# The first 128 rows of the last block's first product move in front of a branch, and the last expert's sums get a bank each

## The chip, the cores and the metric

The kernel runs on one core of one Trainium2 chip. A core has five engines that run side by side and wait for each other through semaphores: TensorE (PE, matrix products; its weight loads are shown as PEld), VectorE (DVE), ScalarE (ACT), GpSimd (POOL) and SyncE (SP, which issues transfers). PE writes its results into PSUM, a memory of eight banks of 2 KB for each of its 128 partitions; DVE and ACT read them there and write to SBUF, from which PE takes its operands. Each engine has an instruction stream of its own, so a branch in the program is a branch on every engine. The metric is the device time in microseconds (us) from start to end; lower is better.

## The reference, cut to what matters

Three stages follow each other: a recurrent attention over 2 x 768 tokens, a mixture of 8 experts with a limited capacity, and a last block that is applied to every token.

```python
def _moe_ref(x, w_gate, w1, w2, capacity):
    ...                                   # every token goes to the expert of its largest logit
    h = np.maximum(np.einsum('ecd,edf->ecf', disp, w1), 0.0)
    y = np.einsum('ecf,efd->ecd', h, w2)
    ...

def _moe2_ref(x, w_in, w_out, g_ln):      # x: 1536 x 384, w_in: 384 x 1024, w_out: 1024 x 384
    h = x @ w_in
    h_max = np.max(h, axis=-1, keepdims=True)
    e = np.exp(h - h_max)
    sm = e / (np.sum(e, axis=-1, keepdims=True) + 1e-09)
    solu = h * sm
    mu = np.mean(solu, axis=-1, keepdims=True)
    var = np.mean((solu - mu) ** 2, axis=-1, keepdims=True)
    ln = (solu - mu) / np.sqrt(var + 1e-06) * g_ln
    return (ln @ w_out).astype(np.float32)
```

## The kernel before, in words

Every float32 matrix is kept as a high and a low part, and a product is three products: high by high, high by low, low by high. The experts come one after the other. Each has up to 224 rows here (`W`), and its 1024 hidden columns are taken in four quarters, numbered `g` from 0 to 31 over the eight experts. `mm1(g)` makes a quarter of the hidden layer (`hps`), ACT and DVE split it into `hh` and `hl`, and `mm2(g)` adds that quarter's share to the expert's result `yps`: for each of the three blocks of 128 result columns (`dd`) six matmuls, 18 in all. `yps` of an expert is two PSUM tiles: one of two column blocks that share a bank, one of the third. After the fourth quarter ACT copies each tile to the high part of the result (line 820, `yThi`), and DVE subtracts to get the low part (line 821, `yTlo`). The result stands transposed, `yT`: `yThi2` and `yTlo2` hold the first two column blocks, `yThi1` and `yTlo1` the third.

Beside this, `decode_piece` turns the last block's weights, which arrive as 64-bit patterns, into high and low parts piece by piece on DVE and ACT (16 pieces; 0 to 7 are `w_in`, 8 to 15 `w_out`).

An expert with more than 224 tokens needs extra work, `overflow()`. It stands under an `if` on the largest count; with these inputs the branch goes around it. Line 1122 is that branch. On every engine the code ahead of it, the code under it and the code behind it lie one after the other, and on the way around each engine first runs a few semaphore instructions that stand for what the code under the `if` would have counted; engines that wait for results from ahead of the branch wait, behind it, for these counts too.

`solu_block()` stands behind the branch. It first decodes piece 15 (the last of `w_out`). Then it goes over 12 tiles of 128 rows, two tiles ahead with the first product: `h2(t)` is `x @ w_in` for tile `t`, 18 matmuls of 512 columns; `norm1(t)` finds the row's maximum (line 989, DVE); `norm2(t)` is the exponential (line 1001, ACT), the weighting (line 1007, DVE) and the centring (line 1012, POOL); `norm3(t)` is the variance; `flip(t)` transposes (line 1037, PE) and splits; `out2(t)` is the second product. Tile 0 has its maximum and exponential in two halves, from two tiles of one bank each; the other tiles have one tile of two banks, of which there are two in turn, so `h2(3)` cannot start before DVE has finished line 1007 of tile 1.

The order on each engine is the order in which the code is written. PE's first tiles behind the branch are h2(0), h2(1), h2(2), flip(0), h2(3), flip(1), out2(0), h2(4); DVE's are piece 15, norm1(0), norm2(0), norm1(1), norm2(1).

Of the kernel before, what the change touches and what calls it, by code (L numbers as in the profile page):

```python
# [8 lines left out]
F32 = mybir.dt.float32  # L9
# [10 lines left out]
N, DM, NE, DF = B * S, H * D, 8, 1024  # L20
# [3 lines left out]
KD = DM // 128  # L24
KF = DF // 128
W = 224
# [9 lines left out]
def rwkv_moe_solu_kernel(  # L36
# [31 lines left out]
    V, S, G, T = nc.vector, nc.scalar, nc.gpsimd, nc.tensor  # L68
# [32 lines left out]
    raw_t, w1s, w2s, xe = {}, {}, {}, {}  # L101
# [576 lines left out]
    def experts_and_solu():  # L678
# [6 lines left out]
        ps_b = mctx.enter_context(tc.tile_pool(name="ps_b", bufs=2, space=PSUM, **pt))  # L685
        ps_t = mctx.enter_context(tc.tile_pool(name="ps_t", bufs=4, space=PSUM, **pt))

        yT = [[ytp.tile([128, n, YW], F32R, name=f"yT{x}{n}") for n in (2, 1)] for x in ("hi", "lo")]
# [3 lines left out]
        def col(x, kk, sl):  # L692
            return yT[x][kk // 2][:, kk % 2, sl]
# [87 lines left out]
        al = slice(None)  # L781
        hq = {}
# [21 lines left out]
        def mm2(g):  # L804
            e, q = divmod(g, 4)
            if q == 0:
                yps[e] = [ps_b.tile([128, n, W], F32, tag=f"b{n}", name=f"yps{e}_{n}") for n in (2, 1)]
            if q == 1:
                starts_of[e] = reg(e) if e else 0
            for dd in range(KD):  # L810
                for f in range(2):
                    mm3(
                        yps[e][dd // 2][:, dd % 2], w2s[g], hq[g], (al, f, slice(dd * 128, dd * 128 + 128)), (al, f),
                        q == 0 and f == 0 and dd != 1, q == 3 and f == 1,
                    )
            if q == 3:
                start = starts_of.pop(e)
                for n, src in enumerate(yps.pop(e)):
                    hi, lo = (yT[x][n][:, :, bass.ds(start, W)] for x in range(2))
                    S.activation(hi, src, AF.Copy)  # L820
                    V.tensor_tensor(lo, src, hi.bitcast(F32), ALU.subtract)
            w2s.pop(g)
            hq.pop(g)

        def reg(j):
            return nc.values_load(
                starts_i[0:1, j:j + 1], engines=(ENG.Activation, ENG.DVE), min_val=0, max_val=N,
                skip_runtime_bounds_check_because="prefix sums of clipped counts",
            )
# [67 lines left out]
        for g in range(NQ + 2):  # L897
# [27 lines left out]
            if g % 2 == 0 and g:  # L925
                j = g // 2
# [38 lines left out]
        def h2(t):  # L965
            if t == 0:
                ps = [ps_t.tile([128, 512], F32, tag="t", name=f"h2_{t}_{j}") for j in range(2)]
                h2p[t] = ps
            else:
                ps = ps_b.tile([128, 2, 512], F32, tag="b", name=f"h2_{t}")  # L970
                h2p[t] = [ps.rearrange("p a f -> p (a f)")]
                ps = [ps[:, j] for j in range(2)]
            ts_ = slice(t * 128, (t + 1) * 128)
            for j in range(2):
                fs = slice(j * 512, (j + 1) * 512)
                for i, (x, w) in enumerate(((0, 0), (0, 1), (1, 0))):
                    for kk in range(KD):
                        T.matmul(  # L978
                            ps[j], col(x, kk, ts_), wi[w][:, kk, fs], start=not (i or kk), stop=i == 2 and kk == KD - 1,
                        )  # L980
# [78 lines left out]
        def solu_block():  # L1059
            nc.sync.dma_start(out=inv_sb, in_=inv.rearrange("(m p) o -> p m o", p=128)[:, :, 0])  # L1060
            for _ in decode_piece(2 * NP - 1):
                pass
            for t in range(-2, NM):
                if t + 2 < NM:
                    h2(t + 2)
                    norm1(t + 2)
                if t < 0:
                    norm2(t + 2)
                    continue
                for i in range(t + 1 if t else 0, min(t + 2, NM)):  # L1070
                    norm3(i)
                flip(t)
                if t + 2 < NM:
                    norm2(t + 2)
                if t:
                    out2(t - 1)
            out2(NM - 1)

        def overflow():
            load_ids(0, NE, 2, NB)  # L1080
            for e in range(NE):
                ost = reg(NE + e)
                wv = []
                for kind, src in ((1, w1), (2, w2)):
                    for hf in range(2):
                        t = rawp.tile([128, 1536], F32, tag="raw", name=f"ow{kind}_{e}_{hf}")
                        nc.sync.dma_start(out=t, in_=src[e, :, hf])
                        wv.append(t.rearrange("p (q a f) -> p q a f", q=2, a=4 - kind))
                for o in range(NOV):
                    xo = load_xe(e, 2 + o, 1)  # L1090
                    ps = ps_t.tile([128, KD, 128], F32, tag="t", name=f"oxt{e}_{o}")
                    for kk in range(KD):
                        T.transpose(ps[:, kk], xo[:, 0, kk * 128:(kk + 1) * 128], ident)
                    xt = xe_p.tile([128, KD, 128], F32, tag="xhi", name=f"oxs{e}_{o}")
                    V.tensor_copy(xt, ps)
                    hps = ps_b.tile([128, KF, 128], F32, tag="b", name=f"ohp{e}_{o}")
                    for f in range(KF):
                        for kk in range(KD):
                            w = wv[f // 4][:, f // 2 % 2, kk, f % 2 * 128:f % 2 * 128 + 128]
                            T.matmul(hps[:, f], w, xt[:, kk], start=kk == 0, stop=kk == KD - 1)  # L1100
                    ho = [h_p.tile([128, 4, 128], F32, tag="hh", name=f"oh{e}_{o}_{j}") for j in range(2)]
                    for j in range(2):
                        S.activation(ho[j], hps[:, 4 * j:4 * j + 4], AF.Relu)
                    yo = ps_t.tile([128, KD, 128], F32, tag="t", name=f"oy{e}_{o}")
                    for dd in range(KD):
                        for f in range(KF):
                            w = wv[2 + f // 4][:, f // 2 % 2, f % 2, dd * 128:dd * 128 + 128]
                            T.matmul(yo[:, dd], w, ho[f // 4][:, f % 4], start=f == 0, stop=f == KF - 1)
                    for n, sl in ((0, slice(0, 2)), (1, slice(2, 3))):
                        hi, lo = (yT[x][n][:, :, bass.ds(ost + 128 * o, 128)] for x in range(2))  # L1110
                        S.activation(hi, yo[:, sl], AF.Copy)
                        V.tensor_tensor(lo, yo[:, sl], hi.bitcast(F32), ALU.subtract)

        return overflow, solu_block, most

    with tc.manual_schedule():
# [62 lines left out]
```

## Time and profile before

| | us |
|---|---|
| median of 3 runs (339.26 to 340.45) | 340.26 |
| the profiled execution's own time | 340.68 |
| its span, from the first to the last instruction | 338.9 |
| PE busy in it | 321.2 (95%) |
| DVE, ACT, POOL busy | 244.2, 190.2, 145.0 |

The profiled execution is 0.42 us above the median of the runs; 1.8 us of it lie outside the span. Times in the rows below are microseconds from the start of the span.

### The profile page before, as it was taken

To read this page: it belongs to the slowest core of one execution; us is meant where nothing else is said; L and a number is where in the kernel's file an instruction comes from. 1 tells how busy PE (TensorE), PEld (TensorE's weight loads), DVE (VectorE), ACT (ScalarE), POOL (GpSimd) and SP (SyncE) were. 2 spreads that over 40 slices of the span, in tenths; PEclk is the share of its full clock that TensorE was granted. 3 is DMA by queue.
4 is the path that set the end of the run, shared out by engine and by line. 5 is a ranking of instruction groups with operands and counts; after the bars stand their busy time and mean duration, and the time that the engine had idled before them with its cause. 6 is when DMAs were issued, how large, how long until landed. Compare 5 with 4: busy or idle time off the path is not lost. (4 is left out here: it accounts for less than half of the span.)

```text
span 338.9 us, 7222 instructions
## 1 busy us (share of the span) xinstructions
PE 321.2 (95%) x2656; PEld 296.6 (88%) x2656; DVE 244.2 (72%) x573; ACT 190.2 (56%) x408; POOL 145.0 (43%) x197
## 2 busy tenths in 40 slices
PE   8999999999999999999999999699999999999990
PEld 3789878888989999999999999588999999999990
DVE  8999999978598989898999897345664444444410
ACT  1556547565559687777787776124644344443420
POOL 7889798851432231414140455304244233333321
PEclk9999999999999999999999999989999999999997
DMA  6988999211986988989888943100000000000010
GB/s 215 391 323 252 342 384 366 78 67 40 327 299 232 291 286 293 279 286 275 280 264 289 279 148 52 8 0 1 2 23 23 25 23 23 25 23 25 23 47 23
DMA packets 20251, 56.22 MB, mean 166 GB/s; under 512 B 6579, under 2 KB 8885, under 8 KB 20213
## 3 DMA queue, kind: packets, MB, share of 16 engines
q1 hardware_dynamic: 16772, 47.67, 40.0%
q0 software_dynamic: 3440, 8.06, 9.6%
q8 instruction: 21, 0.34, 0.4%
q14 instruction: 18, 0.14, 0.1%
HBM read 50.56 MB, written 5.16 MB: 164 GB/s over the span
## 5 line engine op out<-in xcount | busy, mean ns | idle before, releaser
L779 PE MATMUL yps<-hh,wlo 128*128 128x224 f32 x192 | 52.9, 276 | 0.3 <-DMA wlo<-in_w 0.3
L121 DVE TENSOR_TENSOR wlo<-raw,whi 128x768 fp32r<-128x768 f32 x57 | 52.4, 952 | 1.0 <-ACT whi L115 0.7
L777 PE MATMUL yps<-hh,whi 128*128 128x224 f32 x192 | 52.8, 275 | 0.0
L778 PE MATMUL yps<-hl,whi 128*128 128x224 f32 x192 | 52.6, 274 | 0.0
L115 ACT ACTIVATE whi<-raw 128x768 fp32r<-128x768 f32 x64 | 50.8, 840 | 0.0
L1012 POOL TENSOR_SCALAR e<-e,nmu 128x1024 f32<-128x1024 f32 x12 | 13.5, 1125 | 67.8 <-DVE nmu L1011 67.8
L989 DVE TENSOR_REDUCE nm<-h 128x1 f32<-128x1024 f32 (+1 forms) x13 | 14.8, 1140 | 33.9 <-PE h L978 33.9
L779 PEld LDWEIGHTS yps<-hh,wlo 128*128 128x128 f32 x192 | 36.9, 192 | 0.5 <-DMA wlo<-in_w 0.5
L778 PEld LDWEIGHTS yps<-hl,whi 128*128 128x128 f32 x192 | 36.9, 192 | 0.0
L777 PEld LDWEIGHTS yps<-hh,whi 128*128 128x128 f32 x192 | 36.9, 192 | 0.0
L119 POOL DMA_DIRECT2D wlo<-in_w x7 | 6.9, 984 | 69.7 <-ACT wlo L124 69.7
L1046 PE MATMUL o<-w_hi,shi 128*128 128x384 f32 x96 | 33.1, 345 | 0.0
L1048 PE MATMUL o<-w_hi,slo 128*128 128x384 f32 x96 | 32.2, 335 | 0.0
L1047 PE MATMUL o<-w_lo,shi 128*128 128x384 f32 x96 | 32.2, 335 | 0.0
L791 PE MATMUL hps<-xhi,whi 128*128 128x224 f32 x192 | 27.5, 278 | 0.4 <-issue 0.4
L791 PE MATMUL hps<-xlo,whi 128*128 128x224 f32 x192 | 26.7, 275 | 0.0
L791 PE MATMUL hps<-xhi,wlo 128*128 128x224 f32 x192 | 26.6, 274 | 0.0
L791 PEld LDWEIGHTS hps<-xhi,whi 128*128 128x128 f32 x192 | 24.2, 192 | 0.6 <-issue 0.5
L93 POOL DMA_INDIRECT xe<-xs,ids x16 | 17.8, 1115 | 15.4 <-DMA ids<-idx 11.3
L978 PE MATMUL h<-w_hi,yThi 128*128 128x512 f32 x72 | 21.3, 405 | 3.2 <-ACTq L1122 3.0
L791 PEld LDWEIGHTS hps<-xhi,wlo 128*128 128x128 f32 x192 | 24.0, 192 | 0.0
L791 PEld LDWEIGHTS hps<-xlo,whi 128*128 128x128 f32 x192 | 24.0, 192 | 0.0
(183 smaller groups left out, 790.2 us busy)
## 6 DMA issues: line engine op xcount, KB each, us to landing
raw<-in_w SPq DMA_DIRECT2D x32, 768.0 KB
kvr<-in_kvr SPq DMA_DIRECT2D x12, 576.0 KB
rkT<-in_rkT SPq DMA_DIRECT2D x12, 512.0 KB
w<-in_w_in SPq DMA_DIRECT2D x8, 384.0 KB
w<-in_w_out SPq DMA_DIRECT2D x8, 384.0 KB
wlo<-in_w POOLq DMA_DIRECT2D x7, 384.0 KB
xs<-xg SPq DMA_DIRECT2D x12, 192.0 KB
xe<-xs,ids POOLq DMA_INDIRECT x16, 5.9
```

The costliest lines, as they stand in the source:

```text
L93: nc.gpsimd.indirect_dma_start(out=t[0:n, b, :], out_offset=None, in_=xs[0:rows, :], in_offset=bass.IndirectOffsetOnAxis(ap=ids[0:n, e, c: ...
L115: S.activation(hi, raw, AF.Copy)
L121: V.tensor_tensor(lo, raw, hi.bitcast(F32), ALU.subtract)
L777: T.matmul(ps, w[0][ws], x[0][xsl], start=first, stop=False, skip_group_check=True)
L778: T.matmul(ps, w[0][ws], x[1][xsl], start=False, stop=False, skip_group_check=True)
L779: T.matmul(ps, w[1][ws], x[0][xsl], start=False, stop=last, skip_group_check=True)
L791: T.matmul(ps[:, f], w1s[g][i][:, kk, wf], x[j][:, kk], start=not (i or j or f or kk), stop=j == 1 and kk == KD - 1, skip_group_check=True,)
L978: T.matmul(ps[j], col(x, kk, ts_), wi[w][:, kk, fs], start=not (i or kk), stop=i == 2 and kk == KD - 1,)
L989: V.tensor_reduce(nms[j], ps, AX.X, ALU.max, negate=True)
L1046: T.matmul(ps, hi[:, f % 4], wo[0][:, f], start=f == 0, stop=False)
L1047: T.matmul(ps, hi[:, f % 4], wo[1][:, f], start=False, stop=False)
L1048: T.matmul(ps, lo[:, f % 4], wo[0][:, f], start=False, stop=f == KF - 1)
```

## The change

Three things are edited. For the last expert, `yps` becomes three tiles, each in a bank of its own (the third takes the second buffer of the tag `b2`), and each is evicted by itself: three copies on ACT and three subtractions on DVE where there were two. `h2(0)` is called at the end of `experts_and_solu()`, which is ahead of the branch, and no longer in `solu_block()`; its 18 matmuls go column block by column block of `yT` (`kk`), and within each alternate between the two result tiles, so that the last column block is read by the last six alone. The code under the `if` takes its PSUM from the other pool, as the two banks of h2(0) are now in use there. Nothing else moves: piece 15, `norm1(0)` and all that follows stay behind the branch.

```diff
         def mm2(g):
             e, q = divmod(g, 4)
             if q == 0:
-                yps[e] = [ps_b.tile([128, n, W], F32, tag=f"b{n}", name=f"yps{e}_{n}") for n in (2, 1)]
+                ns = (2, 1) if e < NE - 1 else (2, 1, 2)
+                yps[e] = [ps_b.tile([128, n, W], F32, tag=f"b{n}", name=f"yps{e}_{i}") for i, n in enumerate(ns)]
...
+            alone = e == NE - 1
             for dd in range(KD):
+                y = yps[e][dd][:, 0] if alone else yps[e][dd // 2][:, dd % 2]
...
             if q == 3:
                 start = starts_of.pop(e)
                 for n, src in enumerate(yps.pop(e)):
-                    hi, lo = (yT[x][n][:, :, bass.ds(start, W)] for x in range(2))
+                    if alone:
+                        src = src[:, 0]
+                        hi, lo = (yT[x][n // 2][:, n % 2, bass.ds(start, W)] for x in range(2))
+                    else:
+                        hi, lo = (yT[x][n][:, :, bass.ds(start, W)] for x in range(2))
                     S.activation(hi, src, AF.Copy)
                     V.tensor_tensor(lo, src, hi.bitcast(F32), ALU.subtract)
...
             ts_ = slice(t * 128, (t + 1) * 128)
+            if t == 0:
+                for kk in range(KD):
+                    for i, (x, w) in enumerate(((0, 0), (0, 1), (1, 0))):
+                        for j in range(2):
+                            T.matmul(
+                                ps[j], col(x, kk, ts_), wi[w][:, kk, j * 512:(j + 1) * 512], start=not (i or kk),
+                                stop=i == 2 and kk == KD - 1,
+                            )
+                return
...
             for t in range(-2, NM):
                 if t + 2 < NM:
-                    h2(t + 2)
+                    if t + 2:
+                        h2(t + 2)
                     norm1(t + 2)
...
+        h2(0)
         return overflow, solu_block, most
```

How the instructions stand on PE shows what moves. In the kernel before, the last matmuls of the last expert (the third column block of `mm2(31)`) stand right ahead of the branch:

```order
L778 MATMUL yps_1_3527<-hl_3589,whi_31_3546 128x224
L779 MATMUL yps_1_3527<-hh_3588,wlo_31_3547 128x224
L777 MATMUL yps_1_3527<-hh_3588,whi_31_3546 128x224
L778 MATMUL yps_1_3527<-hl_3589,whi_31_3546 128x224
L779 MATMUL yps_1_3527<-hh_3588,wlo_31_3547 128x224
L1122 COMPARE_AND_BRANCH
```

All of h2(0) stood behind the branch. In the changed kernel PE has 18 matmuls of h2(0) between that place and the branch (line 1140 now); the last nine of them and the branch are these, where `h_0_0` and `h_0_1` are the two result tiles:

```order
L985 MATMUL h_0_1_3667<-w_lo_1513,yThi_1507 128x512
L985 MATMUL h_0_0_3666<-w_hi_1511,yTlo_1509 128x512
L985 MATMUL h_0_1_3667<-w_hi_1511,yTlo_1509 128x512
L985 MATMUL h_0_0_3666<-w_hi_1511,yThi_1508 128x512
L985 MATMUL h_0_1_3667<-w_hi_1511,yThi_1508 128x512
L985 MATMUL h_0_0_3666<-w_lo_1513,yThi_1508 128x512
L985 MATMUL h_0_1_3667<-w_lo_1513,yThi_1508 128x512
L985 MATMUL h_0_0_3666<-w_hi_1511,yTlo_1510 128x512
L985 MATMUL h_0_1_3667<-w_hi_1511,yTlo_1510 128x512
L1140 COMPARE_AND_BRANCH
```

The last six of the 18 are the only ones that read the third column block (`yThi_1508`, `yTlo_1510`); behind the branch PE now goes on with h2(1).

ACT, ahead of the same branch, copied two tiles before (the `ISA` rows set the address from the expert's start, which is only known at run time):

```order
L826 TENSOR_LOAD starts_i
L820 ISA
L820 ACTIVATE yThi_1507<-yps_2_3526 128x2x224
L820 ISA
L820 ACTIVATE yThi_1508<-yps_1_3527 128x224
L1122 COMPARE_AND_BRANCH
```

In the changed kernel it copies three:

```order
L833 TENSOR_LOAD starts_i
L827 ISA
L827 ACTIVATE yThi_1507<-yps_0_3526 128x224
L827 ISA
L827 ACTIVATE yThi_1507<-yps_1_3527 128x224
L827 ISA
L827 ACTIVATE yThi_1508<-yps_2_3528 128x224
L1140 COMPARE_AND_BRANCH
```

The first copy now reads what the first six of PE's last 18 expert matmuls complete, the second what the next six complete; DVE's subtractions stand in the same way, three for two.

## Rows read from the trace of the kernel before

**Rows 1.** The page, part 1: busy us, share, instructions of each engine.

```profile
PE 321.2 (95%) x2656; PEld 296.6 (88%) x2656; DVE 244.2 (72%) x573; ACT 190.2 (56%) x408; POOL 145.0 (43%) x197
```

**Rows 2.** Windows: length, busy us (instructions) by engine, granted clock, DMA share, GB/s.

```profile
30.00:60.00 30.00, 28.60 (x376) 25.17 (x374) 27.87 (x95) 18.03 (x59) 25.03 (x27) 1.00 0.94 351
...
215.85:218.88 3.03, 0.00 (x0) 0.00 (x1) 1.87 (x5) 0.82 (x2) 0.00 (x0) 1.00 0.27 8
218.92:222.33 3.41, 3.41 (x8) 2.76 (x9) 1.67 (x3) 0.61 (x1) 0.00 (x0) 0.50 0.02 2
...
234.04:330.00 95.96, 95.96 (x533) 88.76 (x534) 44.52 (x85) 42.34 (x77) 33.27 (x47) 1.00 0.06 23
```

**Rows 3.** Timeline of PE around the branch: start, us, instruction, [idle before <- releaser].

```profile
213.78 0.27 PE L778 MATMUL yps<-hl,whi 128*128 128x224 f32 x1
...
214.90 0.28 PE L779 MATMUL yps<-hh,wlo 128*128 128x224 f32 x1
...
215.57 0.27 PE L779 MATMUL yps<-hh,wlo 128*128 128x224 f32 x1
218.88 1.64 PE L978 MATMUL h<-w_hi,yThi 128*128 128x512 f32 x3 [3.04 <-ACTq L1122]
...
224.72 0.84 PE L978 MATMUL h<-w_hi,yThi 128*128 128x512 f32 x3
```

**Rows 4.** Line 1122, the branch: sequencer instructions by engine, ns min/median/max, first to last start.

```profile
L1122 DVEq EVENT_SEMAPHORE  x2: 21/21/21, 217.6 to 217.7; - x2
L1122 ACTq EVENT_SEMAPHORE  x2: 17/17/17, 218.8 to 218.9; - x2
...
L1122 PEldq COMPARE_BRANCH  x1: 397/397/397, 213.7 to 213.7; - x1
...
L1122 ACTq COMPARE_BRANCH  x1: 68/68/68, 216.5 to 216.5; - x1
L1122 DVEq COMPARE_BRANCH  x1: 84/84/84, 216.9 to 216.9; - x1
```

**Rows 5.** Timeline of ACT around the branch.

```profile
216.03 0.82 ACT L820 ACTIVATE yThi<-yps 128x448 f32 x2 [5.58 <-PE yps L779]
220.04 0.61 ACT L871 ACTIVATE w_hi<-da,g_sb 128x384 fp32r<-128x384 f32 x1 [3.19 <-DVE da L864]
```

**Rows 6.** Timeline of DVE from the branch to tile 1's weighting.

```profile
216.61 0.92 DVE L821 TENSOR_TENSOR yTlo<-yps,yThi 128x448 f32 x2 [4.97 <-ACT yThi L820]
217.86 0.36 DVE L858 TENSOR_SCALAR da<-w 128x384 int32<-128x384 int32 x1 [0.33 <-DVEq L1122]
...
220.69 0.62 DVE L873 SCALAR_TENSOR_TENSOR w_lo<-da,g_sb,w_hi 128x384 fp32r<-128x384 f32 x1 [0.68 <-ACT w_hi L871]
...
224.92 0.69 DVE L989 TENSOR_REDUCE nm<-h 128x1 f32<-128x512 f32 x1 [1.39 <-PE h L978]
...
232.60 1.28 DVE L1007 SCALAR_TENSOR_TENSOR e<-e,es,h 128x1024 f32<-128x1024 f32 x1
```

**Rows 7.** Timeline of PE, then POOL, before h2(3).

```profile
232.88 1.04 PE L1037 MATMUL st<-ident,e 128*128 128x128 f32 x8
234.04 0.93 PE L978 MATMUL h<-w_hi,yThi 128*128 128x512 f32 x3
...
229.95 1.14 POOL L1012 TENSOR_SCALAR e<-e,nmu 128x1024 f32<-128x1024 f32 x1 [14.91 <-DVE nmu L1011]
```

**Rows 8.** Timeline of PE, then ACT, at an earlier expert's last quarter.

```profile
186.16 0.27 PE L779 MATMUL yps<-hh,wlo 128*128 128x224 f32 x1
...
186.55 1.03 ACT L820 ACTIVATE yThi<-yps 128x448 f32 x2 [0.15 <-PE yps L779]
```

**Rows 9.** Groups by shape, whole span: busy us, mean ns of one, idle before.

```profile
L989 DVE TENSOR_REDUCE nm<-h 128x1 f32<-128x512 f32 x2 | 1.4, 692 | 2.9 <-PE h L978 2.9
...
L821 DVE TENSOR_TENSOR yTlo<-yps,yThi 128x224 f32 x7 | 2.7, 382 | 0.0
...
L820 ACT ACTIVATE yThi<-yps 128x224 f32 x7 | 2.5, 358 | 0.7
```

More of the change, by code (lines that the diff above doesn't have):

```diff
@@ L806, in mm2 @@
             if q == 0:
-                yps[e] = [ps_b.tile([128, n, W], F32, tag=f"b{n}", name=f"yps{e}_{n}") for n in (2, 1)]
+                ns = (2, 1) if e < NE - 1 else (2, 1, 2)
+                yps[e] = [ps_b.tile([128, n, W], F32, tag=f"b{n}", name=f"yps{e}_{i}") for i, n in enumerate(ns)]
             if q == 1:
                 starts_of[e] = reg(e) if e else 0
+            alone = e == NE - 1
             for dd in range(KD):
+                y = yps[e][dd][:, 0] if alone else yps[e][dd // 2][:, dd % 2]
                 for f in range(2):
                     mm3(
-                        yps[e][dd // 2][:, dd % 2], w2s[g], hq[g], (al, f, slice(dd * 128, dd * 128 + 128)), (al, f),
-                        q == 0 and f == 0 and dd != 1, q == 3 and f == 1,
+                        y, w2s[g], hq[g], (al, f, slice(dd * 128, dd * 128 + 128)), (al, f),
+                        q == 0 and f == 0 and (alone or dd != 1), q == 3 and f == 1,
                     )
@@ L1090, in overflow @@
                     xo = load_xe(e, 2 + o, 1)
-                    ps = ps_t.tile([128, KD, 128], F32, tag="t", name=f"oxt{e}_{o}")
+                    ps = ps_b.tile([128, KF, 128], F32, tag="b", name=f"oxt{e}_{o}")[:, 0:KD]
                     for kk in range(KD):
@@ L1103, in overflow @@
                         S.activation(ho[j], hps[:, 4 * j:4 * j + 4], AF.Relu)
-                    yo = ps_t.tile([128, KD, 128], F32, tag="t", name=f"oy{e}_{o}")
+                    yo = ps_b.tile([128, KF, 128], F32, tag="b", name=f"oy{e}_{o}")[:, 0:KD]
                     for dd in range(KD):
```

## The prediction

> **What bounds the kernel now.** I read the page first: PE is busy for 95% of the span [rows 1], so only what keeps PE waiting, or slow, can matter. Then the windows: from 234.04 to 330 us PE is never idle [rows 2], so whatever moves the start of h2(3) moves the end by as much, and I need not look behind it. Then PE's timeline at the branch. The last expert matmul starts at 215.57, and the next matmul, the first of h2(0), at 218.88: 3.04 us idle, released by ACT's instructions of the branch line [rows 3]. In that gap the granted clock falls: the first 3.41 us behind it run at 0.50 (the 1.2 GHz level), and the eight matmuls that start there take 3.41 us [rows 2], 0.43 us each, where 36 matmuls of the same shape take 8.16 us from 224.72 to 232.88, 0.227 us each [rows 3, 7]. So the branch costs PE 3.0 us idle and some 1.7 us of half speed.
>
> The gap itself: PE's branch record is at 213.7, when the second of the last 18 matmuls starts (213.78), that is 17 matmuls, each with its weight load, ahead of execution [rows 3, 4]. ACT starts its two copies at 216.03 and ends at 216.85 [rows 5]; its branch record is at 216.5, and its first instruction behind it at 218.8, 2.3 us later [rows 4]. That is what PE waits for. DVE needs no more than 0.7 us, from 216.9 to 217.6 [rows 4].
>
> One thing there is odd, and I shall need it. Where no branch is near, ACT's copy of an expert's result starts 0.39 us behind the start of the last matmul that it needs (186.16 and 186.55) [rows 8]. At the branch the matmul is at 214.90 and the copy at 216.03, 1.13 us behind [rows 3, 5]. 216.0 is also 2.3 us after PE's branch record, the time that ACT's own branch takes. So PE may **hold back its semaphore updates** while it waits for the code behind its branch.
>
> **The change part by part.** *The three banks.* The third sum is complete with the same matmul as before. Its copy may start at 215.57 + 0.39 = 215.96, takes 0.36 and the subtraction 0.38 [rows 9], so DVE is free at 216.7 instead of 216.61 + 0.92 = 217.53 [rows 6]. The first two sums are complete 12 and 6 matmuls earlier, so their copies lie beside PE's work. One copy and one subtraction more cost ACT and DVE nothing that anyone waits for: ACT was idle for 5.58 us before them [rows 5].
>
> *h2(0) in front of the branch.* Its 18 matmuls follow the expert's at once, from 215.7. The third column block is read by the 13th to the 18th, from 215.7 + 12 x 0.227 = 218.4, and its copy and subtraction are done by then. At full clock they end at 215.7 + 18 x 0.227 = 219.8. PE's branch record comes 17 matmuls ahead again, as the second of the 18 is started, at 215.7 to 215.9; with 2.3 us its code is there at 218.2. ACT's record comes with its third copy at 216.0, its code at 218.3. Both lie under h2(0), so both waits are hidden. If that cover were gone, it would be up to 2.3 us again. PE then needs its own last update, some 0.4 us behind the start of its last matmul, and a few semaphore instructions: h2(1) at about 220.3, where it stood at 224.72 [rows 3]. PE is 4.4 us early there.
>
> *What is late next: DVE.* Piece 15 of the weights still stands behind the branch, ahead of the first maximum. It takes DVE and ACT from 217.86 to 220.69 + 0.62 = 221.31, 3.45 us [rows 6]; before, that was hidden by PE's wait and by the slow h2(0). Now DVE goes on at 216.7 + 0.33 (the idle time before 217.86 [rows 6]) = 217.05, or, should its branch need all of the 0.67 us from its record, at 217.3. Piece 15 ends at 220.5 to 220.75. The two maxima of tile 0 are 0.69 us each [rows 9], and as h2(0) completes both halves together, neither can come much before 219.9; they follow piece 15. The second starts at 221.2 to 221.45, where it started at 224.92 [rows 6]: 3.5 to 3.7 us earlier. From there to line 1007 of tile 1 (232.60, ending at 233.88 [rows 6]) the timelines of DVE and ACT name only each other as releasers, so the chain moves as it is. h2(3) waits for the end of line 1007: it started at 234.04, 0.16 us behind it [rows 6, 7], and will start at about 230.4. PE itself could be there at 220.3 + 8.16 + 0.8 (flip(0), with its start bound by POOL's centring, 229.95 + 1.14 less 3.6 = 227.5 [rows 7]) = 229.3. So of PE's 4.4 us some 1.1 are given back as a wait in front of h2(3).
>
> *The sum.* 3.6 us of the profiled execution's 340.68, so 337.1; that execution is 0.42 us above the median of the runs, so 340.26 - 3.6 = **336.7 us**. If DVE did not get free any sooner than 217.86, the gain would still be 224.92 - (221.31 + 0.69) = 2.9 us; if piece 15 cost nothing, PE's 4.4 us and the 0.4 us that it now loses before h2(3) would bound it, 4.8 us. I take 3.6, since the piece is in the program.
>
> The Trainium skill ("Advanced Engine Details and Errata", "Engine Queue Depths") gives TensorE a queue of 64 instructions, which would be 32 matmuls with their weight loads. By it the branch record would come 14 matmuls before h2(0) begins, about 214.1, and with updates held for 2.3 us all three copies would start behind 216.4, the gain some 2.7 us by my estimate. The trace shows 17 matmuls, 34 instructions [rows 3, 4], and the sum goes by that.
>
> *No cost taken.* The bank that the third sum takes was the previous expert's; in the order of the code that expert's copies stand a whole `mm1` ahead of its first use, and an expert's copies are short (0.36 us for one column block) [rows 9]. The alternation between two banks I take at the rate of h2(1); the end of the range for it is the half-speed rate of 0.43 us [rows 2].
>
> **The rivals.** *Held updates.* If PE posts no update between its branch record and the arrival of its code, the update for the third copy, due at about 215.9, falls just behind the record and comes only at 218.0 to 218.1. The copy and the subtraction then end at 218.9, DVE starts piece 15 at 219.2, ends it at 222.65, and the second maximum starts at 223.3: a gain of 1.6 us, **338.6 us**. ACT's code arrives at 220.4, just as PE wants h2(1). For it: the copy at 216.03 [rows 5]. Against it: that record was 1.2 us older when the first held update was due, while here the update is due 0.2 us after the record, perhaps before the holding begins.
>
> *The clock falls once more.* PE's new waits, 0.5 us behind h2(0) and 1.1 in front of h2(3), are shorter than the 3.04 us after which the clock fell [rows 3]. If it falls all the same, half speed costs 1.7 us again: 338.4 with prompt updates, **340.3**, no change, with held ones, where PE waits for over 2 us in front of h2(3).
>
> *The alternation slows PE: the slower end.* Every matmul of h2(0) writes another bank than the one before. If that put the clock at its lower level, h2(0) would take 18 x 0.43 = 7.7 us, to 223.4, and the 3.41 us behind it would run at 0.50 as they do now [rows 2], another 1.7 us; h2(1), h2(2) and flip(0) would end at 223.4 + 0.5 + 8.16 + 1.7 + 0.8 = 234.6, 0.5 us after the present start of h2(3): **340.8 us**, slower. It decides once PE loses more than the 4.8 us that it can gain. Against it: in the attention stage the scores' matmuls also write two banks in turn, and the clock is 1.00 from 30 to 60 us [rows 2], though those have 128 columns and not 512. The Trainium skill ("TensorE: Matmul & The Clock Gate", "A second HAM failure mode: psum-queue depth-cycling") tells of a kernel that went round the PSUM banks with 512 columns each and whose clock swung between its two levels; no run here shows it.
>
> **How the numbers follow.** Prompt updates, 336.7: 0.60 (its own range 335.9 to 337.4, from gains of 4.4, all that PE has at h2(1), and 2.9). Held updates, 338.6: 0.22. The clock once more: 0.06 with prompt updates, 0.08 with held ones. The alternation: 0.04. The range 335.9 to 339.0 reaches over the held updates and the fallen clock with prompt ones, and leaves out the last two, 0.12. About 0.5% (1.7 us, a border at 338.56) is what a measurement of this kernel can tell from no change. The held case lies on that border and is divided: faster 0.60 + 0.11 + 0.05 = 0.76; same 0.11 + 0.01 + 0.08 = 0.20; slower 0.04.
>
> **What would show it.** Right: no idle time before the first matmul of h2(0); 0.227 us from one to the next; a granted clock of 1.00 from 215 us on; the third copy at about 216.0; h2(1) near 220.3 and h2(3) near 230.4 with DVE's line 1007 as releaser. The held case shows the third copy near 218.1 and piece 15 from 219.2. The prediction would be wrong if PE met its branch late (a gap of up to 2.3 us behind h2(0)), or if DVE or ACT had to fetch code for longer than they did here.

## The result, and the profile of the changed kernel

| | before | changed |
|---|---|---|
| median of 4 runs each, us | 340.36 (339.26 to 341.25) | 336.87 (336.36 to 337.07) |
| profiled execution: own time, span, us | 340.68, 338.9 | 336.87, 335.1 |
| mean granted clock of the span | 0.989 | 0.993 |

The ratio is 0.9897 (95%: 0.9866 to 0.9928): 3.5 us gained, where 3.6 were predicted. The page's first part, to be set against [rows 1], shows PE with 1.8 us less busy time:

```profile
PE 319.4 (95%) x2656; PEld 295.3 (88%) x2656; DVE 244.0 (73%) x574; ACT 190.4 (57%) x409; POOL 145.9 (44%) x197
```

The windows (length, busy us of PE, PEld, DVE, ACT and POOL, granted clock, DMA share, GB/s) answer to [rows 2]: the clock is 1.00 where 3.41 us ran at 0.50.

```profile
216.00:219.50 3.50, 3.50 (x18) 2.85 (x16) 2.64 (x6) 0.35 (x2) 0.00 (x0) 1.00 0.28 13
219.50:230.00 10.50, 9.70 (x46) 7.61 (x44) 6.84 (x17) 4.27 (x11) 1.14 (x1) 1.00 0.00 1
```

PE's timeline, against [rows 3, 7]. The last expert matmul (214.69) is followed by h2(0) in nine rows of two matmuls, then h2(1) (line 994 at 220.28), flip(0) (line 1053) and h2(3):

```profile
214.69 0.27 PE L779 MATMUL yps<-hh,wlo 128*128 128x224 f32 x1
215.50 0.73 PE L985 MATMUL h<-w_hi,yThi 128*128 128x512 f32 x2 [0.54 <-ACT yThi L827]
...
218.81 0.62 PE L985 MATMUL h<-w_lo,yThi 128*128 128x512 f32 x2
219.26 0.61 PE L985 MATMUL h<-w_hi,yTlo 128*128 128x512 f32 x2
220.28 0.93 PE L994 MATMUL h<-w_hi,yThi 128*128 128x512 f32 x3 [0.41 <-PEq L1140]
...
228.57 1.03 PE L1053 MATMUL st<-ident,e 128*128 128x128 f32 x8
230.25 0.94 PE L994 MATMUL h<-w_hi,yThi 128*128 128x512 f32 x3 [0.65 <-DVE e L1023]
```

The idle time of 3.04 us has become three short ones: 0.54 ahead of h2(0), 0.41 ahead of h2(1), 0.65 ahead of h2(3). Two matmuls of h2(0) take 219.26 - 218.81 = 0.45 us. ACT's timeline, against [rows 5]: three copies in one piece, all behind the last expert matmul.

```profile
215.09 1.04 ACT L827 ACTIVATE yThi<-yps 128x224 f32 x3 [5.51 <-PE yps L779]
219.27 0.62 ACT L878 ACTIVATE w_hi<-da,g_sb 128x384 fp32r<-128x384 f32 x1 [3.15 <-DVE da L871]
```

DVE's, against [rows 6]: the subtractions, piece 15 (lines 865 to 880), both maxima of tile 0.

```profile
215.48 1.12 DVE L828 TENSOR_TENSOR yTlo<-yps,yThi 128x224 f32 x3 [4.72 <-ACT yThi L827]
217.10 0.36 DVE L865 TENSOR_SCALAR da<-w 128x384 int32<-128x384 int32 x1 [0.50 <-DVEq L1140]
...
219.93 0.62 DVE L880 SCALAR_TENSOR_TENSOR w_lo<-da,g_sb,w_hi 128x384 fp32r<-128x384 f32 x1 [0.69 <-ACT w_hi L878]
220.46 1.28 DVE L1005 TENSOR_REDUCE nm<-h 128x1 f32<-128x512 f32 x2
```

The branch, line 1140 now, against [rows 4]: ACT, DVE and PE meet it under h2(0) (215.50 to 219.87).

```profile
L1140 ACTq EVENT_SEMAPHORE  x2: 17/17/17, 217.8 to 217.9; - x2
...
L1140 ACTq COMPARE_BRANCH  x1: 68/68/68, 215.7 to 215.7; - x1
L1140 DVEq COMPARE_BRANCH  x1: 84/84/84, 216.2 to 216.2; - x1
L1140 PEldq COMPARE_BRANCH  x1: 397/397/397, 216.7 to 216.7; - x1
```

One caution before the times are compared: the last expert matmul starts at 214.69 here and at 215.57 before [rows 3]. That 0.88 us lies ahead of h2(0) and of the branch; over the 14 profiles of this study that start lies between 214.69 and 216.34, and for the two kernels themselves at 215.57 and 215.93 (before), 214.69, 215.76 and 215.31 (changed). So from here on the stage is measured from that start. By this measure h2(3) starts at 18.47 before and at 15.56 now: the change itself gave 2.91 us in these two profiles, and behind h2(3) nothing differs (338.9 - 234.04 = 104.9 and 335.1 - 230.25 = 104.9 us).

### The profile page after: what moved, and what is told of

It is laid out like the page before. It is cut to its first block, busy times and chain, and to the rows that moved or that the text cites. A ratio compares the mean times of both kernels' runs of the same rounds, so it can differ in the third digit from the quotient of the medians.

```text
span 335.1 us, 7226 instructions
## 1 busy us (share of the span) xinstructions
PE 319.4 (95%) x2656; PEld 295.3 (88%) x2656; DVE 244.0 (73%) x574; ACT 190.4 (57%) x409; POOL 145.9 (44%) x197
## 5 line engine op out<-in xcount | busy, mean ns | idle before, releaser
L1028 POOL TENSOR_SCALAR e<-e,nmu 128x1024 f32<-128x1024 f32 x12 | 13.6, 1129 | 64.9 <-DVE nmu L1027 64.9
L93 POOL DMA_INDIRECT xe<-xs,ids x16 | 18.5, 1156 | 14.6 <-PE xt L770 6.6
L798 DVE SCALAR_TENSOR_TENSOR hl<-hps,hh 128x448 fp32r<-128x448 f32 x32 | 19.8, 619 | 5.1 <-ACT hh L797 5.1
```

The costliest lines, as they stand in the source:

```text
L93: nc.gpsimd.indirect_dma_start(out=t[0:n, b, :], out_offset=None, in_=xs[0:rows, :], in_offset=bass.IndirectOffsetOnAxis(ap=ids[0:n, e, c: ...
L798: V.scalar_tensor_tensor(hl, ps, 0.0, hh.bitcast(F32), ALU.max, ALU.subtract)
```

## The experiments

Twelve runs were made, in three groups of four, each group on one chip, beside runs of the kernel before on the same chip. The table gives, for every profile, four times less the start of the last expert matmul in the same profile. Copies that start 0.37 us behind the matmuls that complete their sums are called prompt below (the first number is then negative; in piece_early, where ACT had just decoded piece 15, the first copy starts 0.68 us behind its matmul and the third 0.37), copies that come together behind the last matmul late.

| profile | group | first copy starts | subtractions end | maxima of tile 0 end | h2(3) starts |
|---|---|---|---|---|---|
| before | - | 0.46 | 1.96 | 10.04 | 18.47 |
| changed | - | 0.40 | 1.91 | 7.05 | 15.56 |
| banks_only | 1 | -0.96 | 1.16 | 6.89 | 15.33 |
| move_only | 1 | -0.30 | 1.20 | 6.33 | 14.83 |
| piece_early | 1 | -0.66 | 1.15 | 5.49 | 15.50 |
| post | 1 | -0.97 | 1.15 | 6.33 | 14.82 |
| before_again | 2 | 0.31 | 1.81 | 9.59 | 18.02 |
| after_again | 2 | 0.59 | 2.11 | 7.24 | 15.73 |
| piece_late | 2 | 0.36 | 1.87 | 6.27 | 14.75 |
| old_order | 2 | 0.59 | 2.10 | 7.24 | 15.73 |
| after_2 | 3 | -0.97 | 1.15 | 6.34 | 14.84 |
| post_2 | 3 | -0.97 | 1.15 | 6.33 | 14.82 |
| spare | 3 | -0.97 | 1.15 | 6.55 | 15.04 |
| piece_split | 3 | -0.97 | 1.15 | 5.49 | 13.98 |

**First group** (before: 338.81 us, median of 35 runs). *banks_only* is the kernel before with the edit of `mm2` alone:

```diff
-                yps[e] = [ps_b.tile([128, n, W], F32, tag=f"b{n}", name=f"yps{e}_{n}") for n in (2, 1)]
+                ns = (2, 1) if e < NE - 1 else (2, 1, 2)
+                yps[e] = [ps_b.tile([128, n, W], F32, tag=f"b{n}", name=f"yps{e}_{i}") for i, n in enumerate(ns)]
...
```

> The kernel before with the three banks alone; h2(0) stays behind the branch in its old order. Theory (the sums' copies are not released before the last expert matmul has run, bank or no bank): all three copies start within 0.3 us of each other, behind the start of the last expert matmul, DVE is free about 1.9 us behind that start as in the kernel before, PE's gap stays at 3.0 us and the half-speed matmuls behind it too: 340.4 us, ratio 0.998 to 1.002. Rival (a bank of its own releases each copy as its sum is complete): the first two copies start 0.4 us behind the matmuls that complete them, 1.3 and 0.7 us before the last one; the third copy and ACT's branch record come 0.4 to 0.8 us sooner, the gap shrinks to some 2.3 us: 339.7 us, ratio 0.998 or lower.

Measured: 337.64 us, ratio 0.9974 (0.9948 to 1.0000). The profile looks as the rival has it: the first two copies start 0.96 and 0.36 us ahead of the last expert matmul, and the gap is half of that of [rows 3]. ACT's first copy, PE at the branch line (1129 here), PE's timeline, then the window behind the gap:

```profile
214.00 0.36 ACT L827 ACTIVATE yThi<-yps 128x224 f32 x1 [4.15 <-PE yps L779]
...
L1129 PEldq COMPARE_BRANCH  x1: 392/392/392, 213.1 to 213.1; - x1
L1129 PEldq EVENT_SEMAPHORE  x1: 51/51/51, 215.3 to 215.3; - x1
...
214.96 0.28 PE L779 MATMUL yps<-hh,wlo 128*128 128x224 f32 x1
216.75 0.96 PE L985 MATMUL h<-w_hi,yThi 128*128 128x512 f32 x3 [1.51 <-ACTq L1129]
...
216.75:220.16 3.41, 3.41 (x15) 2.84 (x16) 2.62 (x6) 0.62 (x1) 0.00 (x0) 1.00 0.26 7
```

No half speed follows: 15 matmuls in 3.41 us where [rows 2] has 8. The interval of the runs only just reaches no gain at all. How much of the shorter gap the banks gave is not shown: this chip is a prompt one (move_only below), and the kernel before has a profile on late chips alone. In runs with a mean clock of 0.992 and above the banks gain nothing here (median of 9 runs 337.38 us, of 15 runs of the kernel before 337.43); the lower median comes with fewer runs at a lower clock, 3 of 12 against 20 of 35.

*move_only* undoes that edit in the changed kernel and keeps the move, so that two tiles are copied and subtracted:

```diff
-                ns = (2, 1) if e < NE - 1 else (2, 1, 2)
-                yps[e] = [ps_b.tile([128, n, W], F32, tag=f"b{n}", name=f"yps{e}_{i}") for i, n in enumerate(ns)]
+                yps[e] = [ps_b.tile([128, n, W], F32, tag=f"b{n}", name=f"yps{e}_{n}") for n in (2, 1)]
...
```

> The changed kernel with the last expert's sums in two tiles again (two column blocks in one bank, the third in another); h2(0) stays ahead of the branch, column by column. Theory (the move is the whole gain): 336.9 us plus or minus 0.4; the first copy is 0.1 us longer (448 columns and not 224), so PE's wait ahead of h2(0) grows from 0.54 to some 0.65 us, but two copies and two subtractions together are no longer than three, so piece 15 starts on DVE no later and the second maximum of tile 0 stays where it was. Rival (the three banks carry a part of the gain, by the prediction 0.8 us of it): 337.7 us, with DVE free 0.8 us later.

Measured: 336.74 us, 0.9943 (0.9921 to 0.9965); h2(3) at 14.83. The theory holds: the whole gain of the changed kernel is there without the banks (post and after_2, with three banks and a third copy as early, have h2(3) at 14.82 and 14.84). The last expert matmul and h2(3) on PE:

```profile
215.95 0.28 PE L779 MATMUL yps<-hh,wlo 128*128 128x224 f32 x1
...
230.78 0.93 PE L987 MATMUL h<-w_hi,yThi 128*128 128x512 f32 x3 [0.43 <-DVE e L1016]
```

*piece_early* decodes piece 15 ahead of `mm2(31)`:

```diff
+            if g == NQ + 1:
+                for _ in decode_piece(2 * NP - 1):
+                    pass
             if g >= 2 and g not in (4, 5):
                 mm2(g - 2)
...
-            for _ in decode_piece(2 * NP - 1):
-                pass
```

> The changed kernel with piece 15 decoded ahead of the last expert's sums, where DVE has some 5 us of idle time, and not behind the branch. Theory (piece 15 on DVE is what is late behind the branch): the two maxima of tile 0 start as soon as h2(0) has ended, 0.3 to 0.7 us sooner than in the changed kernel, the idle time of PE ahead of h2(3) falls from 0.65 us to under 0.3: 336.3 us, 0.3 to 0.7 below the changed kernel. Rival (the maxima wait for h2(0) anyway, or DVE's branch takes the place of the piece): 336.9 us, PE's wait ahead of h2(3) stays.

Measured: 337.67 us, 0.9961 (0.9929 to 0.9993), about 1 us above move_only and post, though the intervals overlap. The theory's first half is right, the maxima end 0.84 us sooner (5.49 against 6.33). But DVE's timeline has something that neither theory had:

```profile
228.72 1.28 DVE L1026 SCALAR_TENSOR_TENSOR e<-e,es,h 128x1024 f32<-128x1024 f32 x1
231.45 0.08 DVE L1026 DVE_READ_ACCUMULATOR e<-e,es,h 128x1 f32 x1 [1.45 <-issue]
```

DVE stands still for 1.45 us between the weighting of tile 1 and the read of its accumulator, two instructions that always follow each other, with nothing named that it waits for; PE's idle time ahead of h2(3) grows to 1.39 us. That DVE's code was late there, since the move had shifted all code behind it, is a guess: the profile names no releaser. The trace's DMA records are in line with it. A packet of 8 KB on one of the page's two `instruction` queues lands at 230.11, 1.34 us ahead of that read, and in all 14 profiles ACT's semaphore instructions behind the branch start 1.0 to 1.3 us behind the landing of such a packet. Which engine a packet is for is not recorded.

*post* adds one instruction, so that PE posts an update at the end of `mm2(30)`:

```diff
+            if g == NQ - 2:
+                V.memset(hq[g][1][:, 0, 0:1].bitcast(F32), 0.0)
             w2s.pop(g)
```

> The changed kernel with one more small instruction on DVE, a memset of one column of the low part of quarter 30 behind mm2(30): it makes PE post a semaphore update at the end of mm2(30), so that the update with the first of the last three sums stands for some 6 matmuls and no longer for some 42. Theory 1 (the update with the large count is late by itself): the first copy starts 0.4 us behind the matmul that completes its sum, 1.0 us sooner than now, the wait of 0.54 us ahead of h2(0) is gone, DVE is free 0.4 us sooner: 336.4 us. Theory 2 (PE posts no update while its front end stands at an instruction whose wait is open, until its queue has run empty): the three updates come as now, together behind the last expert matmul, the wait of 0.54 us stays: 336.9 us.

Measured: 336.47 us, 0.9948 (0.9927 to 0.9970), first copy 0.97 us ahead of the last expert matmul, as theory 1 had it. But move_only, without the memset, was just as prompt on that chip, so the run proves nothing; post_2 below is the second try.

**Second group** (before: 340.33 us, 26 runs). It asks whether the late copies belong to the kernel. *before_again* and *after_again* are the two kernels unchanged.

> The kernel before, unchanged, profiled once more on the chip of the experiments. In the four runs so far the copies of the last expert's sums came 0.37 us behind the matmuls that complete them; in the two profiles that the prediction was made and judged with they came together behind the last matmul, up to 1.7 us late. Theory 1 (late updates belong to this kernel's code): the first copy starts 0.46 us behind the start of the last expert matmul, PE's gap at the branch is 3.0 us and the matmuls behind it run at half speed, as in the first profile. Theory 2 (late updates belong to an execution or a chip and not to the kernel): the first copy starts 0.3 us ahead of the start of the last expert matmul, ACT's branch record comes some 0.4 us sooner, the gap is 2.2 to 2.6 us, and the clock may not fall.

Measured: 340.59 us in one run. Late again, at 0.31. The clock fell again too, but later: some six matmuls at full speed first, then 3.41 us at half speed. PE's timeline and the window:

```profile
218.80 0.96 PE L978 MATMUL h<-w_hi,yThi 128*128 128x512 f32 x3 [2.60 <-ACTq L1122]
219.60 0.94 PE L978 MATMUL h<-w_lo,yThi 128*128 128x512 f32 x3
220.34 1.48 PE L978 MATMUL h<-w_hi,yTlo 128*128 128x512 f32 x3
...
220.34:223.75 3.41, 3.41 (x10) 2.69 (x9) 1.31 (x2) 0.53 (x1) 0.00 (x0) 0.52 0.00 0
```

> The changed kernel, unchanged, profiled and timed on the chip of the experiments, where the kernel before took 338.8 us. Theory 1 (late updates belong to the code): copies behind the last matmul as in its first profile, a wait of 0.54 us ahead of h2(0), a gain of 2.9 us or more: 335.9 us. Theory 2 (late updates belong to an execution or a chip): all three copies 0.37 us behind their matmuls, no wait ahead of h2(0), DVE free 1.1 to 1.2 us behind the start of the last expert matmul as the prediction had it; the time is that of the run with the memset, 336.5 us plus or minus 0.4, so a gain of 2.3 us on this chip.

Measured: 337.88 us, 0.9916 (0.9889 to 0.9943): 2.9 us by the ratio. Late copies, and a wait of 0.73 us ahead of h2(0). All four kernels of this chip are late, all four of the first were prompt.

*piece_late* moves piece 15 behind `norm1(2)` in `solu_block()`:

```diff
-            for _ in decode_piece(2 * NP - 1):
-                pass
...
                     norm1(t + 2)
+                if t == 0:
+                    for _ in decode_piece(2 * NP - 1):
+                        pass
```

> The changed kernel with piece 15 decoded behind the maximum of tile 2 and not ahead of that of tile 0: behind the branch the number of instructions up to that place stays the same, only their order changes, where the run with the piece ahead of the branch moved all later code of DVE and ACT and met a stop of 1.45 us on DVE that no wait explains. Theory 1 (the piece is what the maxima of tile 0 wait for, and the stop was code that was not there yet): the maxima start as h2(0) ends, line 1023 of tile 1 ends 0.5 to 0.7 us sooner, PE's idle time ahead of h2(3) is under 0.2 us, no stop: 0.5 us below the changed kernel. Theory 2 (the piece's 3.45 us are only moved into the way of flip(0)'s subtraction and the weighting of tile 2): PE waits for these ahead of out2(0) or h2(4), and the time is that of the changed kernel or up to 1 us more.

Measured: 340.34 us, 0.9995 (0.9967 to 1.0023): all of the gain is gone. h2(3) does start 0.98 us sooner than in after_again and without idle time. But ACT, whose order is the order of the code, reaches the piece's copy ahead of the squares and of flip(0)'s copies, and waits there for DVE (ACT's timeline); out2(0) pays (PE's):

```profile
234.54 0.62 ACT L878 ACTIVATE w_hi<-da,g_sb 128x384 fp32r<-128x384 f32 x1 [5.30 <-DVE da L871]
...
238.67 0.44 PE L1062 MATMUL o<-w_hi,shi 128*128 128x384 f32 x1 [2.38 <-DVE slo L1055]
```

The two make 2.38 - 0.98 = 1.40 us of the 2.46 by which the run is above after_again; 6 of its 12 runs also have the lower mean clock (last section).

*old_order* sets the loops of h2(0) back:

```diff
-                for kk in range(KD):
+                for j in range(2):
                     for i, (x, w) in enumerate(((0, 0), (0, 1), (1, 0))):
-                        for j in range(2):
+                        for kk in range(KD):
```

> The changed kernel with h2(0) in its old order: all nine matmuls of the first result tile and then those of the second, so that the third matmul of the 18 already reads the third column block. If the copies come 0.37 us behind their matmuls, the third copy starts 0.38 us and ends 0.74 us behind the start of the last expert matmul, and its subtraction 1.1 us behind it; PE then waits 0.5 us ahead of the third matmul and little ahead of the seventh, and h2(0) ends 0.5 to 0.6 us later; the maxima of tile 0 wait for piece 15 on DVE, which ends later still, so the time stays within 0.3 us of the changed kernel. Rival (the order by column blocks carries a part of the gain): 0.5 us or more above it.

Measured: 337.98 us, 0.9931 (0.9903 to 0.9959), h2(3) at 15.73 as in after_again. The order by column blocks gains nothing on a late chip, where all copies come together; on a prompt chip it was not tried.

**Third group** (before: 338.67 us, 15 runs). *after_2* is the changed kernel unchanged, *post_2* is post once more.

> The changed kernel, unchanged, once more beside the three kernels below, as their control. So far four profiles of one chip had the copies of the last sums 0.37 us behind the matmuls that complete them (prompt), and six profiles of other chips had them together behind the last matmul (late), the kernel before and the changed one among these. If this chip is a late one: first copy at least 0.3 us behind the start of the last expert matmul, a wait of 0.5 to 0.7 us ahead of h2(0), h2(3) 15.5 to 15.8 us behind that start. If it is a prompt one: first copy 0.9 us ahead of that start, no wait ahead of h2(0), DVE free 1.15 us behind that start, h2(3) 14.6 us behind it or 0.3 more.

Measured: 336.60 us, 0.9948 (0.9925 to 0.9970). Prompt: the unchanged kernel that was late on two occasions has its three copies 0.37 us behind their matmuls here (the third at 215.68, its matmul at 215.31). ACT's timeline, DVE's, then PE's:

```profile
214.34 0.36 ACT L827 ACTIVATE yThi<-yps 128x224 f32 x1 [4.15 <-PE yps L779]
214.95 0.36 ACT L827 ACTIVATE yThi<-yps 128x224 f32 x1 [0.25 <-PE yps L779]
215.68 0.36 ACT L827 ACTIVATE yThi<-yps 128x224 f32 x1 [0.37 <-PE yps L779]
...
216.07 0.39 DVE L828 TENSOR_TENSOR yTlo<-yps,yThi 128x224 f32 x1 [0.34 <-ACT yThi L827]
217.01 0.36 DVE L865 TENSOR_SCALAR da<-w 128x384 int32<-128x384 int32 x1 [0.55 <-DVEq L1140]
...
215.31 0.28 PE L779 MATMUL yps<-hh,wlo 128*128 128x224 f32 x1
...
230.15 0.94 PE L994 MATMUL h<-w_hi,yThi 128*128 128x512 f32 x3 [0.72 <-DVE e L1023]
```

So lateness goes with the chip or the session, not with the changed kernel; the kernel before was never profiled on a prompt chip.

> The changed kernel with the memset on DVE that makes PE post an update behind mm2(30), so that no late update stands for more than some 6 matmuls. If the large count is what makes the updates late, the first copy is prompt here on a chip where the control is late, the wait ahead of h2(0) is gone, and the time is 0.3 to 0.6 us below the control. If it is not, copies and time are those of the control, plus or minus 0.3 us. On a chip where the control is prompt it can tell nothing.

Measured: 336.48 us, 0.9929 (0.9907 to 0.9951), all marks those of the control. The large count costs nothing here, and on a late chip it was not tried.

*spare* puts 18 small matmuls ahead of h2(0):

```diff
+        fill = ps_t.tile([128, 512], F32, tag="t", name="fill")
+        for _ in range(18):
+            T.matmul(fill[:, 0:128], ones_b, ones_b, start=True, stop=True)
         h2(0)
```

> The changed kernel with 18 small matmuls (128 columns of bfloat16 into a tile that nobody reads, about 1 us in all) between the last expert matmul and h2(0); none of them waits for another engine. Theory 2 (updates are held while PE's front end stands at an open wait): with the wait of h2(0) 18 matmuls further on, the updates of the first two sums come 0.3 us behind the start of their matmuls, the first copy starts 0.9 us ahead of the start of the last expert matmul and DVE is free 1.15 us behind it, although the control is late. Rival (updates are late for another cause): the copies start together behind the last expert matmul or behind the small ones. The time itself is the control's or up to 0.6 us more, since PE runs the small matmuls first.

Measured: 336.52 us in one run. With a prompt control it can say nothing of held updates. It does show PE's slack: h2(0) starts at 1.10 instead of 0.11, and h2(3) only 0.20 later than in after_2, right behind flip(0).

*piece_split* leaves four DVE steps of piece 15 behind `norm1(2)` and puts the copy and the subtraction behind `norm2(2)`:

```diff
-            for _ in decode_piece(2 * NP - 1):
-                pass
+            last = decode_piece(2 * NP - 1)
...
                     norm1(t + 2)
+                if t == 0:
+                    for _ in range(4):
+                        next(last)
...
                 if t + 2 < NM:
                     norm2(t + 2)
+                if t == 0:
+                    for _ in last:
+                        pass
```

> The changed kernel with piece 15 taken out of the way of the maxima once more: its four first steps on DVE stand behind the maximum of tile 2, and the copy on ACT and the subtraction, which in the last try blocked ACT ahead of the squares and flip(0)'s copies, stand behind the weighting of tile 2. Theory (what the last try lost was ACT's queue, 2.38 us ahead of out2(0), and not DVE's time): h2(3) follows flip(0) without idle time as in the last try, out2(0) waits for nothing, no stop on DVE; h2(3) 14.7 to 14.9 us behind the start of the last expert matmul, 0.6 to 1.0 us below the control. Rival (the steps delay flip(0)'s subtraction by 1.1 us, and the last two come too late for the end of out2(0)): PE waits 0.3 us or more inside out2(0) or ahead of h2(4), and the time is the control's or above.

Measured: 335.55 us, 0.9911 (0.9888 to 0.9934), about 1 us below after_2 (the two intervals just overlap; by the profiles h2(3) starts 0.86 us sooner) and the lowest median of all. The maxima wait for h2(0) itself now (DVE), and h2(3) follows flip(0) directly (PE):

```profile
219.01 1.29 DVE L1005 TENSOR_REDUCE nm<-h 128x1 f32<-128x512 f32 x2 [3.05 <-PE h L985]
...
227.89 1.04 PE L1053 MATMUL st<-ident,e 128*128 128x128 f32 x8
228.79 0.93 PE L994 MATMUL h<-w_hi,yThi 128*128 128x512 f32 x3
```

## Why the prediction was right, and where it was not

**PE as the bound, and h2(3) as the mark: right** for this change: what h2(3) gained, the end gained. It is no rule: in piece_late h2(3) came sooner and PE lost more behind it.

**The third copy at 215.96, DVE free at 216.7, 1.13 us behind the last expert matmul: wrong in the execution that was timed.** It was 1.91, because the updates for all three sums came together behind the last matmul. This is the mis-sized term. The prediction had the price ready: "If DVE did not get free any sooner than 217.86, the gain would still be ... 2.9 us"; measured 2.91. On the prompt chips the term is right to 0.02 us (1.15), and the steps built on it too: h2(3) was predicted at 230.4 - 215.57 = 14.83 and came at 14.82 to 14.84 in move_only, post, post_2 and after_2. The prediction had put DVE's 0.83 us down to the three banks; move_only, with two tiles, has DVE free at 1.20, so on a prompt chip the banks give 0.05 of it.

**That PE may "hold back its semaphore updates while it waits for the code behind its branch": wrong.** In the changed kernel PE's branch record comes at 216.7, behind all three copies, and they are late all the same. In banks_only, on a prompt chip, PE stands between its branch record (213.1) and its first instruction behind it (215.3) while the copies start at 214.00 and 214.60: the updates were posted in that time. What holds them on some chips stays open. The large count and the open wait in front of PE were the theories; after_2 has both and is prompt, so neither is enough alone, and the runs that would tell them apart fell on a prompt chip.

**h2(0) from 215.7 without idle time:** 0.54 us late where the copies are late; no such wait in after_2. **Its end and h2(1):** h2(1) was predicted 4.73 us behind the last expert matmul; 5.59 in the timed kernel, 4.79 in after_2 (220.10 - 215.31).

**No cost for the alternation: right,** 0.45 us for two matmuls at a granted clock of 1.00. The swing of the clock that the Trainium skill describes ("TensorE: Matmul & The Clock Gate", "A second HAM failure mode: psum-queue depth-cycling") does not show in this trace.

**Piece 15 is late next: right.** piece_split takes it out of the way, and the maxima end 0.85 us sooner, h2(3) 0.86; its 13.98 is 4.49 us below the 18.47 of the kernel before, where the prediction gave 4.8 as the bound without the piece. PE's slack ahead of h2(3) was given as 1.1 us; 0.65 measured, 0.72 in after_2.

**PE's branch record 17 matmuls ahead of execution: wrong for the changed kernel, without harm.** It is so again in banks_only, from 213.1 to the last expert matmul at 214.96, at 0.11 us each. But in the changed kernel the record comes at 216.7, with 13 of the 18 still to start, and in after_2 at 216.5, again with 13, where the prediction had 215.7 to 215.9. PE's first instruction behind it comes at 219.9, as h2(0) ends, so PE lost no more than the 0.41 us ahead of h2(1). The Trainium skill's depth of 64 ("Advanced Engine Details and Errata", "Engine Queue Depths") would by estimate be 32 matmuls with their weight loads; no run here shows PE so far ahead.

**The gain of 1.7 us from the half speed: right in size, but not there in every execution.** The prediction read it from one profile (and the clock fell as the gap ended, not in it: [rows 2] has 1.00 for the gap). Each run comes with its mean granted clock, and 3.41 us at half speed are 0.005 of a span. The mean is under 1 in any case, as the clock is at 0.50 again at the very end of the span, where PE has no work left: the changed kernel, with no fall at the branch in any of its three profiles, has 0.992 to 0.996. The runs of the kernel before fall apart by it:

| group | before, clock 0.994 and above | before, 0.989 to 0.991 | changed |
|---|---|---|---|
| 1 | 337.43 (15 runs) | 339.17 (17) | not run |
| 2 | 338.90 (7) | 340.55 (14) | 337.88 (10) |
| 3 | 337.41 (5) | 339.02 (10) | 336.60 (10) |

(Medians in us; 8 of 76 runs were lower than 0.989.) The two columns of before differ by 1.6 to 1.7 us, the prediction's term. Against executions in which the clock held, by this reading of the means, the change gains 0.8 to 1.0 us; against the others 2.4 to 2.7. That 336.87 us came so near the predicted 336.7 is thus in part luck: from the last expert matmul on, the profiled pair gained 2.91 us and not the 3.64 forecast, 0.88 us lay ahead of that, and this pair of kernels gained 3.5 us on the first occasion, some 2.9 in group 2 and 1.8 in group 3, by the ratios.

**Parts of the change.** The move carries the gain. With it in place, the three banks add nothing on a prompt chip, and the order by column blocks nothing on a late one. The banks alone went with a shorter gap of 1.51 us on a prompt chip; that the banks shortened it is not shown, as the kernel before has no profile on such a chip.

## What to carry to other kernels

Work put in front of a branch paid twice here: it covered the wait for the code behind it, and it kept the matmul engine from an idle time behind which its clock may fall. Then look at once for what stands first behind the branch on the engine that is waited for next, and move it by engine, not as one block: each engine's queue runs in the order of the code, so a copy that waits for its input blocks every later one (2.38 us ahead of out2(0) in piece_late, none in piece_split). And a gain read from one profile should be split into what every execution loses and what only some do.

## What the hardware showed that was not expected

**By the mean clocks, the clock fell in some executions and not in others of one kernel,** more often where the profile has a longer gap. Counted are runs with a mean clock under 0.9915; gaps are those of the profiles; that the fall in piece_late, piece_early and banks_only lies behind the gap is not shown, as their profiles have none there. The two gaps of the kernel before are from late chips; of the 49 runs 30 are from prompt ones (30 of 50 there, 19 of 26 on the late one), where its gap was not profiled.

| PE's longest idle time from the last expert matmul on | runs with the lower clock |
|---|---|
| before: 2.60 and 3.04 us | 49 of 76 |
| piece_late: 2.38 | 6 of 12 |
| banks_only: 1.51 | 3 of 12 |
| piece_early: 1.39 | 2 of 12 |
| the other kernels: 0.40 to 0.74 | 0 of 72 |

**Updates come at one place late on some chips.** In six profiles (the first pair, group 2) the copies of the last sums started 0.31 to 0.59 us behind the last expert matmul; in eight (groups 1 and 3) 0.30 to 0.97 us ahead of it. At an earlier expert the late kernel is as prompt as any [rows 8]. Two other numbers go with it: PE's branch instruction took 397 ns in the late profiles and 392 in the prompt ones, and ACT needed 2.0 to 2.3 us for the branch in the late ones, 1.1 to 1.8 in the prompt ones. The instruction packet that ACT's code follows (see piece_early) starts 0.4 to 0.8 us behind ACT's branch record in the late profiles, 0.3 behind it in move_only, and 0.4 ahead of it in the other seven prompt ones.

**An engine can stop without a wait that the profile names:** DVE for 1.45 us in the one profile of piece_early, after its code had been moved.
